# Loading the first weight groups in halves, with a new order of the opening stage

## The chip, the cores and the metric

The kernel runs on one core of a Trainium2 chip (trn2). The metric is the device time of one execution in microseconds; times are medians of several runs. A core has a matrix engine (TensorE, PE in the profile, with its weight loads as PEld), VectorE (DVE), ScalarE (ACT), GpSimd (POOL) and SyncE (SP), whose queue issues nearly all DMAs here.

## The reference

Three parts follow each other. Windowed attention over 4 batches and 8 heads (576 positions, head size 64), the lower four heads with a window of 32, the upper four with every fourth of 128; then a feed-forward layer with a maximum of three products; then a sum over eight experts, weighted by a matrix that is normalised eight times by rows and columns.

```python
scores = scale * np.matmul(q, k.transpose(0, 1, 3, 2))
scores = np.where(masks[None, :, :, :], scores, -1000000000.0)
attn = np.exp(scores - np.max(scores, axis=-1, keepdims=True))
attn = attn / (np.sum(attn, axis=-1, keepdims=True) + 1e-09)
out = np.matmul(attn, v)
...
h = np.maximum(np.maximum(x @ w1, x @ w2), x @ w3)      # 2304 x 512 by 512 x 768, weights in float64
x = (h @ w_out).astype(np.float32)
...
for e in range(E):                                       # E = 8, F = 1024
    h = np.maximum(x @ w1[e], 0.0)
    out += P[:, e:e + 1] * (h @ w2[e])
```

## The kernel before

The attention of batch 0 is computed in an opening stage of its own, four pairs of heads p = 0 to 3. The attention of batches 1 to 3 is spread over the feed-forward units of the batch before (`hooks`). Then come the experts' products, which fill most of the time. The change touches only the opening.

**Loads.** LOADS is a list of words that are issued in this order on SP's queue before any other work: `k` is keys and queries of a pair, `v` its values, `m` the two parts of the mask, `w` the small gate weight, `g` a group of feed-forward weights. The weights of the feed-forward layer are 64-bit numbers; a group holds two chunks of 128 x 512 of them, read as 32-bit words into a tile `cx` of 8 KB in a partition. There are three such tiles; group 3 needs the tile of group 0, and so on.

**Narrowing.** `narrow_ops` turns 64-bit numbers into a pair of 32-bit tiles (high part and remainder) in nine steps c1 to c9, each needing the one before: c1, c3, c4, c6, c7 and c9 on DVE, c2, c5 and c8 on ScalarE. In the opening, chunks 0 to 3 (groups 0 and 1) run through these steps one chunk at a time: c30 is step c3 of chunk 0. Index 4 stands for the whole of group 2, whose first two steps are in the opening too.

**Attention steps of pair p.** S: mask products and scores on PE; M: the row maxima on DVE; X: the exponentials on ScalarE; Ra, Rb: the sums' reciprocals on DVE and the normalisation on POOL; T0 to T2: three groups of three transposes on PE, each evacuated by E0 to E2 on ScalarE or DVE as EVAC says; V0, V1: the products with the values; H and L: the split of a result into a high part (ScalarE) and a remainder (DVE). The name is step, pair, part: T02 is the third group of pair 0, V31 the second half of pair 3; in T02+1 one filler product goes ahead of it.

**Order.** ORDER is written out by hand: within `with tc.manual_schedule()` every engine takes its instructions in the order of the list. An instruction that waits holds up all behind it on its engine. Outside that list PE's order stays that of the program, while the other engines' instructions are placed by a scheduler and may go between the items of the list. `keep_warm` issues filler products on PE ahead of the list. Pairs 1 and 2 take their score tiles from the same four PSUM buffers as the V products; transposes have two buffers of their own.

Behind the list, the first two groups' narrowed values are written back to memory (L778), which frees nothing but goes ahead of group 3's load on SP's queue, and `up(0, 0)` begins: units of 12 products (L443), each with an evacuation by ScalarE (L449) or DVE (L451). The unit 0 needs the split results of all four pairs and chunk 0; units 1 and 2 need chunks 1 and 2.

Of the kernel before, what the change touches and what calls it, by code (L numbers as in the profile page):

```python
# [9 lines left out]
F32 = mybir.dt.float32  # L10
F32R = mybir.dt.float32r
U32 = mybir.dt.uint32
# [5 lines left out]
B, H, S, D = 4, 8, 576, 64  # L18
# [23 lines left out]
STAGES = {0: "S Ma Mb Xe Ra Rb", 6: "W", 8: "T0 E0 T1 E1", 9: "T2 E2", 11: "V0 H0 L0 V1 H1 L1"}  # L42


LOADS = "m0 k0 w0 k1 m2 k2 g0 k3 v0 g1 v1 v2 v3 g2"
EVAC = "AAV VVV VAV AAA".split()
ORDER = (
# [5 lines left out]
)  # L53
NT, DM = B * S, H * D
F1 = 768
# [1 line left out]
P = 128  # L57
# [5 lines left out]
KT = DM // P  # L63
# [36 lines left out]
def attention_moe(ctx: ExitStack, tc: tile.TileContext, q, k, v, mask, wm1, wg, wm2, out):  # L100
    nc = tc.nc
# [13 lines left out]
    raw_p = ctx.enter_context(tc.tile_pool(name="raw", bufs=4))  # L115
    wa_p = ctx.enter_context(tc.tile_pool(name="wa", bufs=8))
    cx_p = tc.alloc_tile_pool(name="cx", bufs=3)
    dram = ctx.enter_context(tc.tile_pool(name="dram", bufs=1, space=bass.MemoryType.DRAM))
    ps_g = tc.alloc_tile_pool(name="ps_g", bufs=4, space=PSUM)
# [18 lines left out]
    def load_qk(b, p, pool):  # L138
        kt = pool.tile([P, S + WIN], F32, name="kt")
        qt = pool.tile([P, NQ, P], F32, name="qt")  # L140
        nc.sync.dma_start(kt, k[b, p])
        nc.sync.dma_start(qt, q[b, p])
        return qt, kt

    def load_v(b, p, pool):
        vt = pool.tile([KW, NQ, P], F32, name="vt")
        nc.sync.dma_start(vt, v[b, p])
        return vt

    def keep_warm(ps, n):  # L150

        for _ in range(n):
            nc.tensor.matmul(ps, ident[:, :ps.shape[0]], ident, start=True, stop=True)
# [209 lines left out]
    def fetch_w1(b, g):  # L363
        raw = raw_p.tile([P, 2, 512], F32, name="raw")
        if b:
            nc.sync.dma_start(raw, wm1f[g])
            return raw, None
        t = cx_p.tile([P, KT * S], U32, name="cx", tag="cx")
        nc.sync.dma_start(t[:, 0:2048].rearrange("p (i n) -> p i n", i=2), wm1[g].bitcast(U32))
        return raw, t  # L370
# [358 lines left out]
    qk, vs, raws = {}, {}, {}  # L729
    for what in LOADS.split():  # L730
        i = int(what[1])
        if what[0] == "k":
            qk[i] = load_qk(0, i, pools[i])
        elif what[0] == "v":
            vs[i] = load_v(0, i, pools[i])
        elif what[0] == "m":
            m0, m1 = (0, BANK0) if i == 0 else (BANK0, BANK0 + NQ * KW)
            nc.sync.dma_start(mraw[:, m0:m1], mask[:QT, m0:m1])
            if i == 0:
                nc.scalar.copy(mr[:QT, m0:m1], mraw[:, m0:m1])  # L740
        elif what[0] == "w":
            nc.sync.dma_start(wgr, wg)
        else:
            raws[i] = fetch_w1(0, i)
    steps = {"r2": lambda: nc.gpsimd.tensor_copy(mr[:QT, BANK0:], mraw[:, BANK0:])}
# [2 lines left out]
            if name not in "W X0 X1 X2 X3 X4 Ma Mb Xe".split():  # L748
                steps[f"{name[0]}{p}{name[1:]}"] = op
    first_w = made[0]  # L750
    keep_warm(ps_g.tile([P, 512], F32, name="ps")[:, 0:P], 8)
    todo = ORDER.split()
    raw, t = raws[2]
    parts = []
# [3 lines left out]
    for i in range(4):  # L758
        raw, t = raws[i // 2]
# [5 lines left out]
    with tc.manual_schedule():  # L765
        for name in todo:
            name, _, idle = name.partition("+")
# [328 lines left out]
    for i, (blk, e, n) in enumerate(stages):  # L1096
        wo, xo = w_ops.pop(i), x_ops[blk]
        raws = ahead_w.pop(i)
# [280 lines left out]
    for g in range((NBLK - 1) * E):  # L1379
        blk, e = 1 + g // E, g % E  # L1380
        sec = Second(blk, e, outs.pop(g))
        for n0 in range(0, NPAIR, 2):
            i = NS + g * NPAIR + n0
# [6 lines left out]
            ps = [[None, None], [None, None]]  # L1390
# [156 lines left out]
```

## Time and profile before

| | before |
|---|---|
| median of 3 runs | 1893.02 us (1892.87 to 1895.89) |
| profiled execution | 1894.94 us |
| its span, first to last instruction | 1893.0 us |
| mean granted TensorE clock | 0.992 |
| PE busy | 1852.9 us, 98% |
| DVE busy | 1335.1 us, 71% |
| ScalarE busy | 978.6 us, 52% |
| POOL busy | 648.7 us, 34% |

Times in the profile are microseconds from the start of the span. Busy times of a stretch are given for each engine; PEclk is the TensorE clock that was granted, 1.00 being 2.4 GHz and 0.50 being 1.2 GHz. A row of the timeline tells when an instruction (or a run of like ones, x their number) began, how long it took, its engine, line and operands, and in brackets how long the engine had been idle and what released it.

### The profile page before, as it was taken

To read this page: it belongs to the slowest core of one execution; us is meant where nothing else is said; L and a number is where in the kernel's file an instruction comes from. 1 tells how busy PE (TensorE), PEld (TensorE's weight loads), DVE (VectorE), ACT (ScalarE), POOL (GpSimd) and SP (SyncE) were. 2 spreads that over 40 slices of the span, in tenths; PEclk is the share of its full clock that TensorE was granted. 3 is DMA by queue.
4 is the path that set the end of the run, shared out by engine and by line. 5 is a ranking of instruction groups with operands and counts; after the bars stand their busy time and mean duration, and the time that the engine had idled before them with its cause. 6 is when DMAs were issued, how large, how long until landed. Compare 5 with 4: busy or idle time off the path is not lost.

```text
span 1893.0 us, 34127 instructions
## 1 busy us (share of the span) xinstructions
PE 1852.9 (98%) x12055; PEld 1745.3 (92%) x12055; DVE 1335.1 (71%) x2531; ACT 978.6 (52%) x2395; POOL 648.7 (34%) x552
## 2 busy tenths in 40 slices
PE   7899999999999999999999999999999999999998
PEld 6799999998899998989999999999989999999997
DVE  6993365677866677667587777877777677776777
ACT  5764445444554544454446555565545545555554
POOL 1123243335666676766512121121211211212111
PEclk8999999999999999999999999999999999999999
DMA  8776485866666668776977767777797676676763
GB/s 258 259 239 228 151 281 203 305 225 225 238 251 259 251 252 296 281 263 246 375 236 249 232 216 229 223 247 236 240 329 254 215 236 221 225 256 213 235 215 100
DMA packets 218441, 458.82 MB, mean 242 GB/s; under 512 B 19936, under 2 KB 102944, under 8 KB 216736
## 3 DMA queue, kind: packets, MB, share of 16 engines
q1 hardware_dynamic: 216640, 454.29, 70.6%
q10 hardware_dynamic: 1632, 2.36, 0.4%
q8 instruction: 96, 1.57, 0.3%
q14 instruction: 73, 0.60, 0.1%
HBM read 325.42 MB, written 130.81 MB: 241 GB/s over the span
## 4 chain that ended last, share of the span: by engine, by line
PE 82%; DVE 9%; DMA 4%; ACT 2%; issue 2%; POOL 1%; SPq 0%; DVEq 0%; ACTq 0%; POOLq 0%
PE po L1316 25%; PE po L1411 12%; PE po L1065 9%; PE ps L443 7%; PE p L1411 6%; PE q L1411 6%; PE q L1111 4%; PE p L1111 4%; PE ps L653 4%; DMA raw<-in_wm 1%; PE ps L573 1%; DVE sums L799 1%; DVE h L1162 1%; DVE ts L838 1%; DMA qt<-in_q 1%
## 5 line engine op out<-in xcount | busy, mean ns | idle before, releaser
L1316 PE MATMUL po<-wt,hop 128*128 128x256 f32 (+1 forms) x3264 | 482.9, 310 | 2.7 <-DMA wt<-wtd 2.7
L1316 PEld LDWEIGHTS po<-wt,hop 128*128 128x128 f32 x3264 | 444.9, 191 | 38.4 <-ACT wt L82 2.9
L83 POOL TENSOR_TENSOR wt<-raw,wt 128x256 fp32r<-128x256 f32 x192 | 186.4, 996 | 757.7 <-ACT wt L82 745.2
L83 DVE TENSOR_TENSOR hop<-r,hop 128x384 fp32r<-128x384 f32 x384 | 208.7, 573 | 188.6 <-ACT hop L82 184.8
L1065 PE MATMUL po<-wb,h 128*128 128x512 f32 x1152 | 295.0, 392 | 0.4 <-POOL wb L83 0.4
L1065 PEld LDWEIGHTS po<-wb,h 128*128 128x128 f32 x1152 | 213.4, 188 | 34.2 <-POOL wb L83 1.1
L82 ACT CAST hop<-r 128x384 fp32r<-128x384 f32 x384 | 188.7, 516 | 56.5 <-DVE r L1292 30.5
L443 PE MATMUL ps<-xt,wa 128*128 128x288 f32 x1296 | 187.0, 301 | 5.4 <-DVE xt L308 3.3
L443 PEld LDWEIGHTS ps<-xt,wa 128*128 128x128 f32 x1296 | 176.0, 190 | 9.2 <-DVE xt L308 3.8
L83 POOL TENSOR_TENSOR wa<-raw,wa 128x256 fp32r<-128x256 f32 (+1 forms) x107 | 130.9, 1228 | 110.7 <-ACT wa L82 87.7
L1425 ACT ACTIVATE r<-r 128x384 f32<-128x384 f32 x192 | 99.8, 525 | 128.9 <-DVE r L1424 128.0
L83 POOL TENSOR_TENSOR tw<-ts,tw 128x512 fp32r<-128x512 f32 x64 | 86.8, 1378 | 93.8 <-DVE h L1162 51.9
L1411 PE MATMUL po<-xB,wa 128*128 128x384 f32 x576 | 116.9, 338 | 0.0
L1411 PE MATMUL po<-xt,wa 128*128 128x384 f32 x576 | 116.9, 338 | 0.0
L1345 DVE SCALAR_TENSOR_TENSOR acc<-po,prob,acc 128x256 f32<-128x256 f32 x222 | 95.1, 475 | 21.6 <-PE po L1316 17.5
L83 POOL TENSOR_TENSOR wa<-sums,wa 128x512 fp32r<-128x512 f32 x64 | 88.0, 1394 | 51.5 <-ACT wa L82 32.9
L1411 PEld LDWEIGHTS po<-xB,wa 128*128 128x128 f32 x576 | 102.5, 188 | 0.0
L1411 PEld LDWEIGHTS po<-xt,wa 128*128 128x128 f32 x576 | 102.5, 188 | 0.0
L83 POOL TENSOR_TENSOR wb<-raw,wb 128x512 fp32r<-128x512 f32 x64 | 93.7, 1464 | 25.3 <-ACT wb L82 24.8
L1286 DVE TENSOR_TENSOR r<-r,r 128x384 f32<-128x384 f32 x128 | 93.2, 728 | 2.2
L799 DVE TENSOR_TENSOR sums<-raw 128x256 f32<-128x256 f32 x64 | 42.5, 663 | 68.6 <-DMA raw<-in_wm 68.6
L1327 ACT COPY mm<-po 128x256 f32<-128x256 f32 x144 | 49.6, 376 | 78.7 <-PE po L1316 78.7
(246 smaller groups left out, 3361.0 us busy)
## 6 DMA issues: line engine op xcount, KB each, us to landing
wa<-wsd SPq DMA_DIRECT2D x192, 512.0 KB, 4.3
wt<-wtd SPq DMA_DIRECT2D x256, 256.0 KB, 3.7
wsd<-wa SPq DMA_DIRECT2D x96, 512.0 KB, 3.3
raw<-in_wm SPq DMA_DIRECT2D x64, 512.0 KB, 4.3
wtd<-tw SPq DMA_DIRECT2D x128, 256.0 KB, 2.8
raw<-in_wm SPq DMA_DIRECT2D x128, 256.0 KB, 5.3
wa<-wsd SPq DMA_DIRECT2D x64, 256.0 KB, 4.6
cx<-in_wm SPq DMA_DIRECT2D x12, 1024.0 KB, 9.5
```

Source lines behind the costliest of these rows:

```text
L82: nc.scalar.copy(hi, src)
L83: sub.tensor_tensor(out=lo, in0=src, in1=hi.bitcast(F32), op=ALU.subtract)
L443: nc.tensor.matmul(ps, w[:, wi, kk], xt[:, xi, kk, n0:n0 + HB], start=(n == 0), stop=(n == 3 * KT - 1),)
L653: nc.tensor.matmul(ps, wo[f][:, wi, d2 * P:(d2 + 1) * P], hs[f][:, hi, a * HB:(a + 1) * HB], start=(f == 0 and n == 0), stop=(f == NF1 - 1 ...
L799: nc.vector.tensor_tensor(out=s[:, o], in0=x, in1=y, op=op)
L1065: nc.tensor.matmul(po, self.hs[f, j][:, hi, t * P:(t + 1) * P], self.ws[f][:, wi], start=(n + f + k == 0), stop=(n == NPAIR - 1 and f == 1 ...
L1111: nc.tensor.matmul(ps, wo[w][:, wi, kk], xo[x][:, xi, kk], start=(first and k == 0), stop=True if k == 5 else False, skip_group_check=not ...
L1286: nc.vector.tensor_tensor(out=r[o, n], in0=r[x, n], in1=r[y, n], op=op)
L1316: nc.tensor.matmul(self.ps[side, t][:, 0:x.shape[-1]], h[:, hi, t * P:(t + 1) * P], x, start=(first and i == 0), stop=(n == NPAIR - 1 and ...
L1345: nc.vector.scalar_tensor_tensor(out=a, in0=src, scalar=g, in1=a, op0=ALU.mult, op1=ALU.add)
L1411: nc.tensor.matmul(ps[k][side], wo[k][w][:, wi, kk], xo[x][:, xi, kk], start=(first and c == 0), stop=c == 5, skip_group_check=not first,)
L1425: nc.scalar.activation(out=r, in_=r, func=AF.Relu)
```

## The change

The two whole loads g0 and g1 become four half loads h0 to h3, one chunk of 512 KB each; the first stands directly behind the first part of the mask and the fourth behind the keys and queries of pair 1. Pair 1 is loaded ahead of pair 0, and the gate weight moves to the end of the list. ORDER is laid out anew: it begins with the narrowing of chunk 0 and the first step of chunk 3, the scores come in the order of pairs 1, 0, 2, 3, and the pairs' transposes, V products and splits are interleaved. The filler products ahead of the list go from 8 to 14. Chunks 0 and 3 are narrowed first, 1 and 2 later; the steps of group 2 (c14, c24) close the list.

```diff
-LOADS = "m0 k0 w0 k1 m2 k2 g0 k3 v0 g1 v1 v2 v3 g2"
+LOADS = "m0 h0 k1 h3 k0 m2 k2 k3 h1 h2 v1 v2 v0 v3 g2 w0"
 EVAC = "AAV VVV VAV AAA".split()
 ORDER = (
-    "S0 M0 X0 S1 M1 r2 R0a R0b X1 S2 M2 c10 c11 T02+1 T01 E02 c20 c21 E01 R1a R1b T00+2 E00 S3 X2 "
-    "c30 c40 c31 V01 V00 M3 R2a R2b c41 c50 T10 T11 E10 E11 T12 E12 c51 H01 H00 V11 V10 c12 X3 c60 c70 c61 "
-    "c71 R3a R3b c22 L01 L00 T20 E20 T21 E21 T22 E22 c80 H11 c81 H10 V21 V20 c90 c32 c42 L11 L10 c91 "
-    "T30+1 E30 T31 E31 T32 E32 c52 H21 H20 c62 L21 c72 L20 V31 V30 H31 c13 c82 H30 c23 L31 c92 c33 c43 "
-    "L30 c53 c14 c24 c63 c73 c83 c93"
+    "c10 c20 c30 c40 c50 c60 c13 S1 c70 M1 c23 c33 c43 c80 c90 S0 r2 S2 M0 X1 c53 R1a c63 X0 c73 M2 R1b "
+    "T11 c83 T12 R0a E11 c93 S3 E12 R0b T01 X2 c11 M3 c21 R2a c31 R2b T02+1 E01 E02 c12 c41 X3 T10 E10 "
+    "T20 V11 T21 E20 R3a T22 c22 E21 H11 c32 c51 R3b V20 E22 V21 H20 H21 L11 c61 c42 T00+2 T31 V10 c71 "
+    "E00 L20 E31 c52 L21 H10 T32 T30+1 V00 E32 E30 c62 c81 L10 c72 V31 H00 V30 c91 L00 H31 L31 H30 L30 "
+    "V01 H01 c82 L01 c92 c14 c24"
 )
...
         elif what[0] == "w":
             nc.sync.dma_start(wgr, wg)
+        elif what[0] == "h":
+            g, n = divmod(i, 2)
+            if g not in raws:
+                raws[g] = (
+                    raw_p.tile([P, 2, 512], F32, name="raw"), cx_p.tile([P, KT * S], U32, name="cx", tag="cx"),
+                )
+            nc.sync.dma_start(raws[g][1][:, n * 1024:(n + 1) * 1024], wm1[g][:, n].bitcast(U32))
         else:
             raws[i] = fetch_w1(0, i)
...
-    keep_warm(ps_g.tile([P, 512], F32, name="ps")[:, 0:P], 8)
+    keep_warm(ps_g.tile([P, 512], F32, name="ps")[:, 0:P], 14)
```

## Rows read from the trace of the kernel before

**Rows 1.** Stages: length, busy PE PEld DVE ACT POOL, PEclk, DMA share, GB/s.

```profile
5.00:10.00 5.00, 3.63 (x25) 2.72 (x23) 1.39 (x3) 0.92 (x6) 0.25 (x1) 1.00 1.03 275
10.00:15.00 5.00, 3.61 (x18) 3.64 (x18) 0.66 (x1) 2.32 (x15) 0.90 (x1) 0.66 1.02 375
15.00:20.00 5.00, 4.06 (x31) 3.24 (x30) 3.59 (x11) 3.84 (x20) 1.63 (x1) 1.00 1.06 293
35.00:40.00 5.00, 4.85 (x47) 3.78 (x45) 2.10 (x6) 2.69 (x8) 0.00 (x0) 0.50 0.99 308
```

**Rows 2.** The same view in stages of 10 us, around the hand-over from DVE to PE.

```profile
90.00:100.00 10.00, 8.46 (x105) 7.81 (x101) 9.85 (x17) 7.54 (x15) 1.87 (x1) 1.00 1.01 330
100.00:110.00 10.00, 9.95 (x102) 9.50 (x102) 10.00 (x20) 9.03 (x31) 1.64 (x1) 1.00 0.82 289
```

**Rows 3.** Timeline, the first landings and score products: start, us, engine line op.

```profile
1.79 3.45 PE L153 MATMUL ps<-ident 128*128 128x128 f32 x16 [1.79 <-POOL ident masks.py:199]
3.48 0.59 ACT L740 CAST mk<-mraw 64x480 fp32r<-64x480 f32 x1 [1.46 <-DMA mraw<-in_mask]
6.18 2.22 PE L190 MATMUL pss<-kt,qt 128*128 128x96 f32 x18 [0.36 <-DMA qt<-in_q]
11.39 3.85 PE L190 MATMUL ps<-kt,qt 128*128 128x96 f32 x18 [2.40 <-DMA qt<-in_q]
12.51 0.90 POOL L745 CAST mk<-mraw 64x864 fp32r<-64x864 f32 x1 [5.62 <-DMA mraw<-in_mask]
```

**Rows 4.** Timeline, narrowing steps of chunks 0 and 1 and a normalisation.

```profile
18.73 0.75 DVE L344 TENSOR_SCALAR raw<-cx 128x512 uint32<-128x512 uint32 x2
19.18 1.33 ACT L347 ACTIVATE raw<-raw,ebias 128x512 uint32<-128x512 uint32 x2
20.41 1.89 POOL L256 TENSOR_TENSOR sm<-sm,st 128x864 f32<-128x864 f32 x1 [2.27 <-DVE st L253]
20.85 1.74 DVE L351 TENSOR_SCALAR cx<-cx 128x512 uint32<-128x512 uint32 x1
24.80 0.37 DVE L351 TENSOR_SCALAR cx<-cx 128x512 uint32<-128x512 uint32 x1
28.16 0.69 DVE L358 TENSOR_TENSOR raw<-raw,cx 128x512 f32<-128x512 f32 x1
```

**Rows 5.** Timeline, V products and transposes, and the end of the opening.

```profile
23.69 1.27 PE L284 MATMUL ps<-pt,vt 96*64 96x64 f32 x36
24.89 0.86 PE L267 MATMUL pst<-ident,sm 128*96 128x128 f32 x6
29.89 1.52 PE L267 MATMUL pst<-ident,sm 128*96 128x128 f32 x6
38.79 1.98 PE L284 MATMUL ps<-pt,vt 96*64 96x64 f32 x32 [0.15 <-ACT pt L271]
45.41 0.61 PE L443 MATMUL ps<-xt,wa 128*128 128x288 f32 x2 [2.41 <-DVE xt L308]
45.26 1.29 DVE L344 TENSOR_SCALAR raw<-cx 128x1024 uint32<-128x1024 uint32 x2
47.80 2.35 DVE L348 SCALAR_TENSOR_TENSOR raw<-cx,raw 128x1024 uint32<-128x1024 uint32 x2
50.07 0.68 DVE L341 TENSOR_TENSOR wa<-raw,wa 128x512 fp32r<-128x512 f32 x1
```

**Rows 6.** DMA issues up to 60 us: op xcount, KB each, us to landing.

```profile
cx<-in_wm SPq DMA_DIRECT2D x6, 1024.0 KB, 12.1
qt<-in_q SPq DMA_DIRECT2D x6, 576.0 KB, 8.6
kt<-in_k SPq DMA_DIRECT2D x6, 304.0 KB, 7.2
mraw<-in_mask SPq DMA_DIRECT2D x1, 216.0 KB, 8.6
mraw<-in_mask SPq DMA_DIRECT2D x1, 120.0 KB, 2.7
```

## The prediction

> **What bounds the kernel now.** I read the table of stages first: engine time, granted TensorE clock and DMA rate in stretches of five and ten microseconds [rows 1]. Between 5 and 15 us VectorE (DVE) works 1.39 + 0.66 us of 10 while the DMA engines are full, so the kernel opens by waiting for its inputs. Past the opening the picture turns: between 90 and 100 us DVE is busy 9.85 of 10 and TensorE (PE) 8.46; from 100 us on PE is busy 9.95 of 10 [rows 2]. So the opening and the first 60 us of the feed-forward stage are limited by DVE (it narrows the 64-bit weights in the steps c1 to c9 and also evacuates PE's results), and the rest of the 1893 us by PE. What the change can win is therefore what DVE and PE have in hand when the opening ends, at about 45 to 50 us; nothing behind that is touched.
>
> The timeline shows how the opening runs. PE fills time with 16 small products until 5.2 us, then takes head pair 0 at 6.18, and pair 1 only at 11.39, released by the landing of its queries after 2.40 us of idling [rows 3]. DVE takes up the first weight step c1 at 18.73 [rows 4]. The opening ends with PE's first feed-forward unit waiting 2.41 us for the last DVE split L30 (45.41) and with DVE finishing c93 at 50.07 + 0.68 = 50.75 us. By then DVE has also done work that is not in ORDER: one of the two steps in the row at 45.26 (0.64 us) and both wide steps in the row at 47.80 (2.35) [rows 5]. Its own share of the opening thus ends at 50.75 - 3.0 = about 47.8 us. That is the figure to compare with.
>
> **When things land.** Bytes and queue are the same, only the order differs; the four half loads move what two whole ones did. Sizes are in [rows 6]. The landings of before give a curve of KB in queue order against time [rows 3]: m0 (120 KB) released ScalarE at 3.48; m0 + k0 (1000) released PE at 6.18; with w0 and k1 1896 KB at 11.39; with m2 2112 KB at 12.51. Past that I go on at 375 GB/s to 15 us, at 293 to 20 [rows 1], and by an estimate at the same 293 behind it. On this curve the new list lands: h0 (632 KB in all) at 5.05, k1 (1512) at 9.1, h3 (2024) at 12.05, k0 (2904) at 14.7, m2 at 15.3, k2 (4000) at 18.4, k3 at 21, h1 and h2 at 23 and 25. A half load has rows of 4 KB in place of 8; no row shows them apart. They lie between those of the keys and those of the whole loads, so I take the curve as it stands, with 1 us either way.
>
> **DVE's gain at the front.** A chunk costs DVE c1 0.375 (0.75 for two), c4 0.37, and c3, c6, c7, c9 at 0.69 each as the c7 row shows: 3.5 us; ScalarE's steps take 0.67 each (1.33 for two) [rows 4]. In the new order chunk 0 starts at 5.05 and comes to c60 at 5.05 + 0.375 + 0.67 + 0.69 + 0.37 + 0.67 + 0.69 = 8.5. There c13 stands in DVE's queue ahead of c70 and M1 and waits for h3 until 12.05: 3.5 us idle, with c70, M1 and everything else behind it, but M1 can't start before S1 is done at 11.4 anyway. Chunk 0 is complete at about 16. So 3.5 + 1.4 (c13, c33, c43) = 4.9 us of DVE work lies where DVE idled before. That is the most that can come out by this step alone.
>
> **PE's path.** The 6 added filler products are 12 instructions at 3.45 / 16 = 0.22 us [rows 3], 2.6 us, until 7.8; they lie in the wait for k1 (9.1) and cost nothing; if k1 came before 7.8 they would cost the difference. S1 then runs 9.1 to 11.4. S0 waits for k0 until 14.7. Before, idling of 2.40 us was followed by pair 1's products at half clock: 3.85 us in place of 2.22 [rows 3], clock 0.66 over 10 to 15 [rows 1]. The new gap is 3.3 us, so I take S0 at half clock, to 18.6; S2 with its 0.6 of mask products at half or full, to 21.4 or 23.1; T11 and T12 0.9; S3 2.9: 25.2 to 26.9. Then ten groups of transposes and four pairs of V products remain. At full clock a group is 0.86 / 2 = 0.43 us and a pair 1.27; at half clock 0.76 and 1.98 x 36 / 32 = 2.2 [rows 5].
>
> Which clock? From 35 to 40 us PE was busy 4.85 of 5 with nothing but such transposes and V products and the granted clock stayed at 0.50, the lower of its two levels, 1.2 GHz [rows 1]. So this kind of work doesn't bring the clock back, and with score products no longer among it I expect the fall soon after S3. The half-clock price is 10 x 0.76 + 4 x 2.2 + 0.7 of filler = 17.1; with the first two or three groups still at full clock, 16: PE ends at 41.2 to 44. Waits for evacuations add about 1: I take 43.7. At full clock throughout it is 10 x 0.43 + 4 x 1.27 + 0.4 = 9.8: PE would end at 35 to 36.7 and DVE would set the end.
>
> The Trainium skill (TensorE: Matmul & The Clock Gate, "Part 4: PE-mode transpose") says that transposes don't count as activity for the clock the way matmuls do. By that rule the new order's second half, mixing them with V products, stays at half clock; the trace agrees with its 0.50 over 35 to 40 us. By the opposite reading, where a busy PE is a fast PE, the full-clock sum would hold.
>
> **A stall that moves.** The normalisation Rb on GpSimd (POOL) ran from 20.41 for 1.89 us, and the c4 that DVE began at 20.85 took 1.74 us, ending with it, where the same step alone took 0.37 [rows 4]. In the new order every one of the four Rb has c steps beside it (c73, c93, c12, c32) where before one had. Each can cost up to 1.37 us, so the price is between 0 and 3 x 1.37 = 4.1 us more; most fall while DVE would wait for PE, and I count 0.8.
>
> The Trainium skill (SBUF — State Buffer, "Who interferes with whom") has the two engines share a port pair under an exclusive lock, for steps with two SBUF inputs as well. The 1.74 us of this c4 agrees; no run yet shows it for c7 or c9. It speaks against the change; by it the stall would come near 4.1, without it to 1.37 or less.
>
> **The sum.** Behind PE's end stand H01, L01, c92 and c14 on ScalarE and DVE: two splits and two steps at about 0.4, 0.4, 0.69 and 0.65, some 2.1 us. DVE's opening ends at 43.7 + 0.8 + 2.1 = 46.6 against 47.8: 1.2 us earlier. PE comes to its first unit 3 us later than before (43.7 against 38.79 + 1.98 = 40.8 [rows 5]), but before it could not finish that unit until 45.41 + 0.61, and it has gaps (1.5 us in 90 to 100 alone [rows 2]) to make up. The third group's load and the write-back wait for c71 and c72; the former DVE position of c61 and c71 was about 28 to 30 and is now about 35, but the queue has earlier loads until then. I take 1.0 us of the 1.2 through to the end.
>
> The profiled execution took 1894.94 us with a span of 1893.0, the median of the runs is 1893.02. The sum is a difference of spans; set against the median it gives 1893.0 - 1.0 = 1892.0.
>
> **The rivals.** (1) The clock holds: score products spread between transposes keep PE at 2.4 GHz to the end. PE's work, done by 36.7, is no longer last. DVE has 26 items of the list behind M3, which ends near 28 (S3, the evacuations and a stall): eleven c steps at 0.375 to 0.69, nine splits and two sums, four evacuations, by estimate 0.53 each, 13.7 us, without a wait: 42 us, 5.8 earlier, less about 0.8 for the next group's load landing late: 1888.0. For it: the clock was 1.00 over 15 to 20 us with the same mix; against it: 35 to 40 [rows 1]. A fall that comes late in the stage lands between, at about 1889.
>
> (2) The clock doesn't come back at all after the gap at 11.4. S2 and S3 take 3.85 each, PE reaches the end of V01 at about 47 and its first feed-forward units run at half clock: 47 + 2.8 by estimate, twelve products somewhat below the pace of the two in 0.61, = 49.8, where before it was 45.41 + 0.61 = 46.0 [rows 5]. PE is 4 us late: 1897. It decides from the point where PE's end of the opening passes about 45.5, when the later gaps no longer take it up. For it: the gap of 3.3 us. Against it: before, 3.85 us of score products brought the clock back.
>
> (3) The change doesn't do what it says: the half loads land no earlier (8 KB rows were cheaper, or the first 5 us are latency). Then c10 starts past 7, the gain at the front is 2 us less and the end stands as before: 1893.
>
> **How the numbers follow.** Forecast with (3), both within 0.2% (3.8 us, about what a measurement of this kernel can tell from no change): 0.50. Rival (1) with its late falls, to 1885 at the best landing: 0.31, most of it past 3.8 us: faster 0.30. Rival (2): 0.19, slower 0.18; what is left adds to same: 0.52. The range takes in the middle of (1) and the price of (2): 1886.5 to 1897. The likeliest case's own range is 1890 to 1894.5.
>
> **What would show it.** In the profile of after: c10 near 5 us and DVE waiting for h3 until 12; PE released by the queries of pair 1 near 9 and of pair 0 near 14.7; the granted clock of 28 to 43 (0.5 is my step, 1.0 rival 1) and of 15 to 26 (0.5 is rival 2); c steps beside an Rb at over 1.3 us; the end of L30 and c92 against 46. I am wrong if DVE is no longer busy past 95% up to 100 us, or if the loads of groups 3 and 4 land after DVE asks for them.

## The result and the profile after

The changed kernel takes 1906.42 us (median of 6 runs, 1905.48 to 1909.22), the kernel before 1893.86 us: a ratio of 1.0068, 95% interval 1.0055 to 1.0081. It is slower by 12.6 us; 1892.0 was forecast, and the range ended at 1897. The profiled execution took 1908.67 us with a span of 1906.7, that of before 1894.94 with 1893.0: 13.7 us more in both ways of counting.

Where the 13.7 us lie can be read from the start of each twelve-product unit of L443, the same units in the same order in both traces (unit 108 is the first behind them, of L573). The table gives this start in the changed kernel minus that in the kernel before, worked out from the timeline.

| unit | start before | after minus before |
|---|---|---|
| 1 | 47.75 | -1.49 |
| 4 | 53.24 | -2.09 |
| 7 | 61.54 | +1.92 |
| 8 | 63.49 | +6.08 |
| 13 | 79.61 | +1.86 |
| 16 | 87.53 | +6.12 |
| 24 | 106.89 | +4.77 |
| 25 | 109.32 | +11.02 |
| 31 to 47 | 121.84 | +11.95 |
| 48 | 174.64 | +10.62 |
| 108 | 340.79 | +13.59 |

In these two executions the opening is a success: units 1 to 4 start 1.5 to 2.1 us early. Then the stage loses 8 us by unit 8, takes 4 back by unit 13, loses them again by unit 16, and loses 6 us more at unit 25. All of that is at 55 to 120 us, behind the lines that the change edits.

The timeline of the opening in the changed kernel (start, us, engine, line, operation; in brackets the idle time and what ended it):

```profile
1.79 5.18 PE L153 MATMUL ps<-ident 128*128 128x128 f32 x28 [1.79 <-POOL ident masks.py:199]
6.36 0.43 DVE L344 TENSOR_SCALAR raw<-cx 128x512 uint32<-128x512 uint32 x1 [4.30 <-DMA cx<-in_wm]
8.92 2.22 PE L190 MATMUL ps<-kt,qt 128*128 128x96 f32 x18 [1.37 <-DMA qt<-in_q]
10.65 0.43 DVE L344 TENSOR_SCALAR raw<-cx 128x512 uint32<-128x512 uint32 x1 [0.49 <-DMA cx<-in_wm]
14.47 2.91 PE L190 MATMUL pss<-kt,qt 128*128 128x96 f32 x18 [2.75 <-DMA qt<-in_q]
18.32 4.15 PE L190 MATMUL ps<-kt,qt 128*128 128x96 f32 x18
18.65 1.88 POOL L256 TENSOR_TENSOR sm<-sm,st 128x864 f32<-128x864 f32 x1 [2.29 <-DVE st L253]
19.08 2.00 DVE L358 TENSOR_TENSOR raw<-raw,cx 128x512 f32<-128x512 f32 x1
```

These answer [rows 3] and [rows 4]. c10 starts at 6.36 us where the first weight step of before started at 18.73, and pair 1's scores start at 8.92 in place of 11.39. The last two rows are one event: c7 of chunk 3, 0.69 us alone [rows 4], takes 2.00 us beside the normalisation on POOL and ends 0.55 us behind it (21.08 against 20.53).

Stages of the changed kernel (length, then busy time of PE, PEld, DVE, ACT, POOL, granted clock, DMA share, GB/s):

```profile
30.00:35.00 5.00, 4.22 (x37) 3.15 (x37) 2.92 (x8) 1.53 (x8) 1.89 (x1) 0.50 1.00 287
35.00:40.00 5.00, 4.61 (x52) 4.09 (x54) 3.39 (x9) 3.67 (x11) 0.25 (x1) 0.53 0.44 141
40.00:45.00 5.00, 5.00 (x101) 4.64 (x96) 4.37 (x11) 4.45 (x13) 0.00 (x0) 1.00 0.98 338
60.00:70.00 10.00, 3.74 (x14) 3.39 (x15) 10.00 (x15) 7.19 (x26) 0.00 (x0) 0.68 0.69 260
80.00:90.00 10.00, 5.00 (x33) 4.72 (x33) 10.00 (x14) 6.82 (x21) 0.00 (x0) 0.87 0.62 210
90.00:100.00 10.00, 10.00 (x129) 9.65 (x129) 9.99 (x17) 7.96 (x19) 2.40 (x1) 0.95 0.97 342
110.00:120.00 10.00, 4.25 (x30) 3.98 (x30) 10.00 (x19) 6.77 (x23) 3.92 (x1) 0.91 0.39 141
120.00:130.00 10.00, 10.00 (x87) 9.67 (x86) 5.99 (x10) 5.14 (x13) 0.00 (x0) 0.75 0.00 0
```

Two of these stages in the kernel before:

```profile
60.00:70.00 10.00, 8.43 (x60) 7.50 (x59) 10.00 (x16) 5.37 (x11) 1.64 (x1) 1.00 0.98 348
110.00:120.00 10.00, 10.00 (x104) 9.77 (x102) 10.00 (x17) 6.74 (x17) 0.00 (x0) 1.00 0.72 259
```

This is the picture that misleads. PE was busy 8.43 us of 10 in 60 to 70 us and 10.00 in 110 to 120; now it is busy 3.74 and 4.25. Yet DVE, the engine that bounds this stretch, is busy 10.00 of 10 in both stages, before and after. It isn't short of work; it works on what PE doesn't need yet. What PE waits for, 45 to 130 us of the changed kernel (engine, tile, line, releaser: total, times, longest):

```profile
PE pst L267 <- POOL sm L256: 5.7, 1, 5.7
PE ps L443 <- ACT wa L337: 5.0, 1, 5.0
PE pst L267 <- DVE xt L308: 5.0, 1, 5.0
PE ps L443 <- DVE wa L341: 2.8, 1, 2.8
PE pss L184 <- DMA qt<-in_q: 1.2, 1, 1.2
PE pst L267 <- ACT pt L271: 0.3, 1, 0.3
```

They sum to 20.0 us, against 11.1 us in the same view of the kernel before, of which 2.4 end at 45.41, still inside unit 0. Four waits make 18.6 of them. They are found in PE's timeline:

```profile
63.47 0.75 PE L443 MATMUL ps<-xt,wa 128*128 128x288 f32 x2 [5.03 <-ACT wa L337]
67.01 4.71 PE L443 MATMUL ps<-xt,wa 128*128 128x288 f32 x22 [2.80 <-DVE wa L341]
88.23 1.48 PE L267 MATMUL pst<-ident,sm 128*96 128x128 f32 x6 [5.00 <-DVE xt L308]
119.17 1.51 PE L267 MATMUL pst<-ident,sm 128*96 128x128 f32 x6 [5.75 <-POOL sm L256]
```

Unit 7 is the first that uses a tile of group 2. Its first product waits for the high part, c8 (L337); its third is the first that needs the remainder and waits for c9 (L341). With the long waits come times at half clock: 0.68 over 60 to 70 us, 0.87 over 80 to 90, 0.75 over 120 to 130. A mean of 0.68 means 6.4 of 10 us at 0.50. Worked out in this way, the last five rows of the changed kernel give 16.8 us at half clock; in the kernel before, 3.4 of 45 to 50 us (clock 0.66) and 3.4 of 70 to 80 us (0.83). The clock is the smaller part of the loss all the same. From the end of unit 0 to the start of unit 31 the changed kernel takes 12.6 us longer (45.35 to 133.79 us, before 46.02 to 121.84). PE's busy time in this stretch is 68.42 us, before 67.08, so 1.3 us are slower work and 11.3 us are idle time.

Why is the weight late although DVE never rests? DVE's timeline in the changed kernel; L344, L355, L358, L341 are c1, c6, c7, c9:

```profile
51.68 0.69 DVE L344 TENSOR_SCALAR raw<-cx 128x1024 uint32<-128x1024 uint32 x1 [0.16 <-DMA cx<-in_wm]
54.87 2.49 DVE L348 SCALAR_TENSOR_TENSOR raw<-cx,raw 128x1024 uint32<-128x1024 uint32 x1
57.28 1.21 DVE L355 SCALAR_TENSOR_TENSOR cx<-cx 128x1024 f32<-128x1024 uint32 x1
61.55 1.21 DVE L358 TENSOR_TENSOR raw<-raw,cx 128x1024 f32<-128x1024 f32 x1
66.28 1.28 DVE L341 TENSOR_TENSOR wa<-raw,wa 128x512 fp32r<-128x512 f32 x2
68.69 0.68 DVE L341 TENSOR_TENSOR wa<-raw,wa 128x512 fp32r<-128x512 f32 x1
71.54 1.75 DVE L341 TENSOR_TENSOR wa<-raw,wa 128x512 fp32r<-128x512 f32 x1
```

and in the kernel before:

```profile
55.37 0.68 DVE L344 TENSOR_SCALAR raw<-cx 128x1024 uint32<-128x1024 uint32 x1
57.10 1.22 DVE L358 TENSOR_TENSOR raw<-raw,cx 128x1024 f32<-128x1024 f32 x1
61.31 1.28 DVE L341 TENSOR_TENSOR wa<-raw,wa 128x512 fp32r<-128x512 f32 x2
```

The first row of each is c1 of group 4. In the changed kernel it stands at 51.68, ahead of the c6 and c7 of group 2; before, it stood behind group 2's c6. So three groups (2, 3, 4) advance abreast and their last steps all lie between 66.28 and 73.29: the rows of L341 at 66.28, 68.69 and 71.54 belong to groups 2, 3 and 4. Before, the c9 of group 2 stood at 61.31, 5 us earlier. Of these 5 us, 1.3 are the c3 of group 4 in the row at 54.87, which took 2.49 us in place of 1.21 beside an Rb on POOL (from 54.65, 1.63 us). The sum of DVE's work is hardly larger: up to 120 us it was busy 102.7 us, before 100.9.

### The profile page after: what moved, and what is told of

The parts are those of the page before. It is cut to its first block, busy times and chain, and to the rows that moved or that the text cites. A ratio compares the mean times of both kernels' runs of the same rounds, so it can differ in the third digit from the quotient of the medians.

```text
span 1906.7 us, 34156 instructions
## 1 busy us (share of the span) xinstructions
PE 1854.8 (97%) x12067; PEld 1749.4 (92%) x12067; DVE 1336.6 (70%) x2531; ACT 981.4 (51%) x2395; POOL 651.2 (34%) x552
## 4 chain that ended last, share of the span: by engine, by line
PE 82%; DVE 8%; DMA 6%; ACT 2%; issue 2%; POOL 1%; SPq 0%; DVEq 0%; ACTq 0%; POOLq 0%
PE po L1323 25%; PE po L1418 12%; PE po L1072 9%; PE ps L443 7%; PE p L1418 6%; PE q L1418 6%; PE q L1118 4%; PE p L1118 4%; PE ps L653 3%; DMA raw<-in_wm 1%; PE ps L573 1%; DVE sums L806 1%; DVE ts L845 1%; DVE h L1169 1%; DMA cx<-in_wm 1%
## 5 line engine op out<-in xcount | busy, mean ns | idle before, releaser
L443 PE MATMUL ps<-xt,wa 128*128 128x288 f32 x1296 | 188.0, 302 | 7.8 <-ACT wa L337 5.0
L443 PEld LDWEIGHTS ps<-xt,wa 128*128 128x128 f32 x1296 | 177.7, 192 | 10.7 <-ACT wa L337 5.3
```

Of the source, the lines that this page charges most:

```text
L443: nc.tensor.matmul(ps, w[:, wi, kk], xt[:, xi, kk, n0:n0 + HB], start=(n == 0), stop=(n == 3 * KT - 1),)
```

## The experiments

Twelve kernels ran, in three sets; each set shares runs of the kernel before, whose median was 1894.61, 1894.70 and 1893.95 us. Ratios are against these.

**Is it the opening or the sequence behind it?** The placement of the feed-forward instructions on DVE and ScalarE, which nobody wrote by hand, differs between the two builds. In e1 and e2 it is prescribed: each of the 213 instructions of DVE and 227 of ScalarE gets an edge from the one ahead of it, in the sequence that the other kernel's build had.

```diff
+            own = [x for x in traced if str(x.engine).endswith(name)]
+            for i, j in zip(at, at[1:]):        # at: the other build's sequence
+                tc.add_manual_dep(own[j], own[i].name, ..., reason="order")
```

e1, the new opening with the feed-forward sequence of before:

> The changed kernel, with the 213 VectorE and 227 ScalarE instructions of the feed-forward stage of batches 0 and 1 put back into the sequence they have in the kernel before (order edges only, no added work). Theory A: the loss is that the change altered that sequence, and the opening itself gained some 2 us. Then the unit that waited at 58.4 to 67.0 us waits under 2 us, and the time is 1889 to 1894, about that of before or 1 to 4 us less. Rival B: the loss is in the opening (its loads, clock or buffers), and the sequence only follows it. Then the time stays near 1906, within 3 us.

1897.17 us, ratio 1.0010 (0.9999 to 1.0021): the loss is gone, but the time lies above theory A's 1889 to 1894, and a gain of the opening doesn't show.

e2, the old opening with the feed-forward sequence of the changed kernel:

> The kernel before with its own loads and opening, but with those 213 and 227 instructions in the sequence of the changed kernel. Theory A: it is slow as well, 1903 to 1911 (10 to 17 us over before), with TensorE waiting over 5 us for group 2's weights and twice again later. Rival B: it stays within 3 us of before, 1891 to 1897.

1907.73 us, ratio 1.0068 (1.0046 to 1.0090), the loss of the change itself, with the opening of before. Its units stand at +6.17 (8), +9.77 (25) and +9.67 us (48), like those of the changed kernel. The two together settle it: the loss is the sequence behind the opening. With the old sequence the new opening can't be told from the old one.

**What in the sequence?** e3 keeps the changed kernel and adds one rule, with all else left to the scheduler:

```diff
+            if name == "c1" and g - 2 in narrowed:
+                with tc.issue_after(narrowed[g - 2]):    # c9 of the group two ahead
+                    op()
```

> The changed kernel with one rule added in the feed-forward stage: VectorE's first step of group g stands behind its last step of group g-2, so that at most two weight groups are in narrowing at once. Theory A in its narrower form (three groups narrowed in step, so that none is done when TensorE needs it): half or more of the 13 us comes back, 1890 to 1899. If another part of the sequence than the number of groups in progress does it, or under rival B: 1902 to 1908.

1895.06 us, ratio 0.9996 (0.9985 to 1.0007). Keeping a third group from starting takes away the whole loss. Its loads of groups 3 and 4 are issued at 37.18 and 41.44 us, as close together as in the changed kernel; so near loads do no harm by themselves, their steps being let in does. The same rule on the kernel before is the control:

> The kernel before with the rule of e3: VectorE's c1 of a group may only be placed behind c9 of the group two ahead of it. A control for e3: if the rule by itself gave several us, then e3 (0.9996 of the kernel before) would hide a loss of that size that remains in the new opening. Theory A: the rule changes little where the sequence is staggered anyway, 1891 to 1896 us. Rival: the rule itself gains, 1885 to 1889.

1894.96 us, ratio 1.0007 (0.9995 to 1.0019): the rule gains nothing by itself that could hide a loss in e3. Its trace also warns how to read unit starts. With the old opening unit 1 starts at 42.84 us, 4.9 earlier than in the trace of before and earlier than in the changed kernel; by unit 48 the lead is 2.2. The granted clock differs too: up to 45 us it was 0.50 for 10.2 us there (30.42 to 37.25 and 40.66 to 44.08) and for 17.1 in the trace of before (11.58 to 14.99 and 28.65 to 42.30). How much of the lead is the clock isn't separated.

**The fillers.** e4 is e1 with 8 filler products in place of 14:

> As the first run, but with 8 filler products in place of 14. If the fillers only lie in the wait for pair 1 and its clock: TensorE's first scores of pair 1 start at the same time, at most at the lower clock for 1.6 us longer, and the end is within 2 us of the first run. If the clock in the opening decides (the fall comes earlier and stays): 3 us or more above the first run.

1896.93 against e1's 1897.17: no difference in the time. In the one traced execution of e4 the scores of pair 1 took 4.13 us, in that of e1 2.22, and unit 1 starts 3.8 us later than in e1; whether the fewer fillers did that isn't shown by one trace of each.

**Which part of the change calls up the bad sequence?** e5 moves four words of the new list:

```diff
-    "E00 L20 E31 c52 L21 H10 T32 T30+1 V00 E32 E30 c62 c81 L10 c72 V31 H00 V30 c91 L00 H31 L31 H30 L30 "
-    "V01 H01 c82 L01 c92 c14 c24"
+    "E00 L20 E31 c52 L21 H10 T32 T30+1 V00 E32 E30 c81 L10 V31 H00 V30 c91 L00 H31 L31 H30 L30 "
+    "V01 H01 L01 c14 c24 c62 c72 c82 c92"
```

> The changed kernel with one edit: in ORDER the steps c62 c72 c82 c92 of the third half chunk (group 1) go from among the transposes to the end, behind c24. Loads, fillers and everything else stay. c72 is the last reader of group 1's raw tile before its write-back, so the load of group 4 (42.54 us in the changed kernel, 4.3 us behind that of group 3) can only start later. The sequence that is built for VectorE behind the opening then has the first step of group 4 behind group 2's c7, no longer ahead of it. Theory A2 (the feed-forward sequence was lost because group 4's weights became ready too early, which let its steps in among those of groups 2 and 3): 1891 to 1897 us, units 25 to 30 no more than 1 us behind the kernel before, where the changed kernel is 11 to 13 us behind. Rival (the sequence is a matter of the opening's length or of group 3's load alone): 1903 to 1908, as changed.

1896.91 us, ratio 1.0012 (1.0002 to 1.0022). Units 8, 25 and 48 stand at -0.18, +0.52 and -0.29. Of the 12.6 us excess, 2.2 are left. The issue rows of SyncE's queue show the step: first in the changed kernel (write-backs of groups 0 and 1, each followed by a load into the buffer that comes free, of groups 3 and 4), then the write-back of group 1 and the load of group 4 in e5, then that load in the kernel before:

```profile
37.88 0.33 SPq L785 DMA_DIRECT2D wm1f<-raw  x1
38.26 0.42 SPq L369 DMA_DIRECT2D cx<-in_wm  x1
42.16 0.33 SPq L785 DMA_DIRECT2D wm1f<-raw  x1
42.54 0.43 SPq L369 DMA_DIRECT2D cx<-in_wm  x1
```

```profile
46.39 0.33 SPq L785 DMA_DIRECT2D wm1f<-raw  x1
48.08 0.49 SPq L369 DMA_DIRECT2D cx<-in_wm  x1
```

```profile
48.29 1.23 SPq L369 DMA_DIRECT2D cx<-in_wm  x1
```

Group 4's load leaves behind the write-back of group 1, which waits for c72. In the changed kernel it leaves at 42.54; in e5 at 48.08, close to the 48.29 of the kernel before. e6 and e7 ask whether it is this time or the distance between the two loads that counts. Both complete group 0 first (loads h0 h1 h2 h3, steps of chunks 0, 1, 2, 3), and differ in four words only:

```diff
-    "E00 L20 E31 c53 L21 H10 T32 T30+1 V00 E32 E30 c63 c82 L10 c73 V31 H00 V30 c92 L00 H31 L31 H30 L30 "
-    "V01 H01 c83 L01 c93 c14 c24"
+    "E00 L20 E31 c53 L21 H10 T32 T30+1 V00 E32 E30 c82 L10 V31 H00 V30 c92 L00 H31 L31 H30 L30 "
+    "V01 H01 L01 c14 c24 c63 c73 c83 c93"
```

e6 (with +, the steps late):

> The changed kernel with the quarters renamed so that group 0 is complete first (loads h0 h1, then h2 h3; steps of chunk 0, 1, 2, 3 in this sequence), and c63 c73 c83 c93 at the end behind c24. Group 0's write-back and with it the load of group 3 then come near 20 us in place of 38, that of group 4 near 50. Theory A2: the sequence of VectorE is staggered as in the kernel before and the load of group 3 no longer ends a wait (in e1 VectorE idled 1.6 us for it), so 1889 to 1895 us. Rival: what the opening gives is taken back at unit 15 whatever is done, because VectorE's work is the same: 1893 to 1897.

1897.10 us, ratio 1.0020 (1.0006 to 1.0034). The loads of groups 3 and 4 leave at 27.07 and 45.30 us and the sequence is staggered, but the time is 0.1 us above the rival's range: DVE waits 1.5 us for loads where it was 1.6 in e1.

e7 (with -, the steps early):

> As e6, but c63 c73 c83 c93 stay among the transposes, where the changed kernel has them. The loads of groups 3 and 4 are then issued some 20 us apart (in the changed kernel 4.3, in the kernel before 17.7), but the second of them as early as in the changed kernel, near 42 us. The sequence built for VectorE again has the first steps of groups 2, 3 and 4 next to one another. Theory A2 (what counts is how early group 4 is ready): 1902 to 1908 us, units 8 and 9 about 6 us behind. Rival A3 (what counts is the distance of the two loads, or that group 3's load was late): 1891 to 1896.

1901.01 us, ratio 1.0035 (1.0020 to 1.0050). The loads of groups 3 and 4 are issued at 26.90 and 39.51 us, 12.6 apart in place of 4.3, and three groups go abreast again; units 8 and 25 are at +2.29 and +6.65. So a wider distance doesn't heal it, though the rival said so; but the loss of 6.3 us is half of the changed kernel's 12.6, and the time just below the range of the theory. With e3 and e5 this shows that group 4's steps, ready early, are what spoils the sequence; by what rule they are placed was read from the built sequences only, and how much the late load of group 3 adds to the price isn't separated.

**Where does the opening's gain go?** In e1 unit 13 starts 6.72 us earlier than in the kernel before, and unit 16 0.20 us later. Not all of this lead is the new order's, since executions differ in their clock: with the same opening list unit 0 starts at 40.79 us in e1, behind 10.2 us at half clock, and at 43.47 in the changed kernel, behind 17.1. In the trace of e1 this is the place where the lead is lost (lines are 17 higher than before: L273 is Rb, L372 c6, L325 a split, L284 a transpose):

```profile
77.28 1.87 POOL L273 TENSOR_TENSOR sm<-sm,st 128x864 f32<-128x864 f32 x1 [16.35 <-DVE st L270]
77.58 2.65 DVE L372 SCALAR_TENSOR_TENSOR cx<-cx 128x1024 f32<-128x1024 uint32 x1
80.16 0.48 DVE L325 TENSOR_TENSOR xt<-pso,xt 128x320 fp32r<-128x320 f32 x1
80.78 1.72 PE L284 MATMUL pst<-ident,sm 128*96 128x128 f32 x6 [6.03 <-DVE xt L325]
```

PE is early, but waits 6.03 us for a split that stands in DVE's sequence behind weight steps, one of them taking 2.65 us beside Rb in place of 1.21. My reading was that DVE's amount of work is the limit. e9 takes 4.2 us of it away in the same sequence: c7 of groups 3 to 6 works on 8 of its 1024 columns and leaves their weights unmultiplied.

```diff
-            "c7": lambda: nc.vector.tensor_tensor(out=dst, in0=dst, in1=mf, op=ALU.mult),
+            "c7": lambda: nc.vector.tensor_tensor(out=dst[:, :few], in0=dst[:, :few], in1=mf[:, :few], op=ALU.mult),
```

> As e1 (the new opening, VectorE's and ScalarE's feed-forward sequence as in the kernel before), but c7 of the groups 3 to 6 works on 8 of its 1024 columns, so four instructions of 1.21 us become short, the sequence staying the same. Their weights are left unmultiplied. Theory (the gain of the opening vanishes in e1 because from 50 to 120 us VectorE's work is the limit): the stage gets back up to 4 x 1.1 = 4.4 us, so 1892.5 to 1895 against e1's 1897.17. Rival (TensorE or the loads are the limit there): 1896 to 1898, as e1.

1895.91 us, ratio 1.0004 (0.9992 to 1.0016), 1.3 us below e1 with intervals that overlap. It lies between the two expectations. The waits of DVE from 45 to 120 us in e9 show what became of the time (L361 is c1, L365 c3, L358 c9, L269 Ra):

```profile
DVE raw L361 <- DMA cx<-in_wm: 2.8, 1, 2.8
DVE st L269 <- ACT sm L254: 1.0, 1, 1.0
DVE raw L365 <- ACT raw L364: 0.8, 2, 0.6
DVE wa L358 <- ACT wa L354: 0.7, 1, 0.7
```

DVE is busy 69.6 us of these 75 in place of 72.8 in e1 (74.7 before): it now waits for a group's load, and for ScalarE. So it isn't DVE's work alone; that a group's load, which has to wait for a buffer and then for the queue, stands right behind it is a reading of these waits. Unit 19 starts at 97.14 us before, 0.19 earlier in e1 and 0.10 earlier in e9. A fourth `cx` buffer would tell the two apart; it wasn't tried.

**A version that beats both?** e10 to e12 give the second c9 of each group from group 3 on to GpSimd, on the kernel before, on e6 and on e5. The sequence of the other steps is left to the scheduler and may change too:

```diff
+                eng = second if second is not None and i else nc.vector    # second: nc.gpsimd
+                eng.tensor_tensor(out=w[:, 1], in0=x, in1=w[:, 0].bitcast(F32), op=ALU.subtract)
```

> The kernel before with the second c9 of every weight group from group 3 on given to GpSimd. VectorE loses 9 steps of 0.767 us between 45 and 125 us, 6.9 us in all; GpSimd takes 1.39 us for one (the 128x512 subtraction elsewhere in the kernel), during which a two-input step of VectorE may stand still: at most 9 x 1.39 = 12.5 us given back. If VectorE's work is the limit and half of the steps collide: 1893.0 - 6.9 + 6.2 = about 1892, between 1888 and 1896. Rival (the collisions are total): 1898. Rival (TensorE is the limit): 1893, whatever VectorE does.

1897.59 us, ratio 1.0017 (1.0007 to 1.0027), above the range of the first expectation and nearest in time to the rival with the total collisions. Groups of DVE's instructions from 45 to 125 us in e10 (L349 is c3, L342 c9, L352 c4, L356 c6; busy, mean ns of one):

```profile
L349 DVE SCALAR_TENSOR_TENSOR raw<-cx,raw 128x1024 uint32<-128x1024 uint32 x9 | 13.5, 1504 | 0.3 <-ACT raw L348 0.3
L342 DVE TENSOR_TENSOR wa<-raw,wa 128x512 fp32r<-128x512 f32 x9 | 10.5, 1172 | 0.0
L352 DVE TENSOR_SCALAR cx<-cx 128x1024 uint32<-128x1024 uint32 x9 | 7.6, 844 | 0.0
L356 DVE SCALAR_TENSOR_TENSOR cx<-cx 128x1024 f32<-128x1024 uint32 x8 | 9.7, 1211 | 0.0
```

In the kernel before these means were 1350, 767, 694 and 1375 ns. Nine c9 that stay take 0.40 us longer each, nine c3 0.15, nine c4 0.15: 6.4 us. Eight c6 take 0.16 less each, 1.3 us, so 5.1 us came back, where the seven steps that POOL did in this stretch freed 7 x 0.767 = 5.4. Nearly all of the work that was moved came back as longer steps; the collisions weren't total, the 6.4 us being well under the 11.0 us that POOL was busy with its seven.

> e6 (quarters in their own order, the last one behind the opening) with the second c9 of every group from group 3 on given to GpSimd. If the opening's gain in e6 was taken back because VectorE's work is the limit up to 120 us, then with 6.9 us less of it the gain should show as far as GpSimd's holding of the shared port allows: 1890 to 1895 against e6's 1897.1. Rival: collisions cost more than 6.9 us: 1898 to 1902.

1895.45 us, ratio 1.0005 (0.9992 to 1.0017): just above the range of the first expectation, below e6, and not told apart from the kernel before.

> e5 (the changed kernel with c62 c72 c82 c92 at the end of the list) with the second c9 of every group from group 3 on given to GpSimd. As e11: 1890 to 1895 against e5's 1896.9 if VectorE's work is the limit and few steps collide; 1898 to 1902 if the collisions cost more than the 6.9 us that are moved.

1901.09 us, ratio 1.0043 (1.0026 to 1.0061): the rival's range. Whether collisions or a changed sequence cost more here isn't separated. None of the twelve is measurably faster than the kernel before.

## Why the prediction was wrong

**The step that failed** is half a sentence: "nothing behind that is touched". The sum took the opening's end, carried 1.0 us of it to the end of the kernel, and left the feed-forward stage as it was. But DVE's instructions outside the list are placed by a scheduler, and the prediction had even counted three of them ahead of the list's last step [rows 5]. A new opening gives that scheduler another start, above all another time for group 4's load, and it lays out the next 70 us anew. The span came out 13.7 us longer, although units 1 to 4 came up to 2.1 us early.

**The marks nearly missed it.** The prediction named as signs of an error DVE below 95% before 100 us, and loads that land after DVE asks. DVE fell below 95% in one stage only, 70 to 80 us, with 8.47 us of 10, behind the first loss and not at its cause; the load of group 4 made DVE wait 0.16 us (51.68). The mark should have been what PE waits for, and which group's step DVE does at that time.

**"The third group's load and the write-back wait for c71 and c72"** was written down, with the price of a later load in mind. What decided was the opposite case, group 4's load 5.75 us earlier (42.54 against 48.29), which looked like a gift.

**The opening's own steps held well.**

| step | predicted | measured |
|---|---|---|
| h0 lands, c10 starts | 5.05 | 6.36 |
| S1 starts (k1) | 9.1 | 8.92 |
| h3 lands, c13 | 12.05 | 10.65 |
| S0 starts (k0) | 14.7 | 14.47 |
| fillers end | 7.8 | 6.97 |
| unit 0 can start | 43.7 | 43.47 |
| last item of DVE's opening ends | 46.6 | about 46.3 (c14, in the row at 45.61) |

The curve of bytes was right within 1.4 us, its stated 1 us being a little narrow. DVE waited for h3 0.49 us where 3.5 was counted, since h0 came later and h3 earlier. Rival 3 is refuted by c10 at 6.36. The instructions of the filler products took 0.185 us each (5.18 / 28) where 0.22 was counted. That PE reached unit 0 at 43.47 for a forecast of 43.7 is partly luck. Behind S3, which ended at 26.03 as forecast, it waited 3.4 us (0.32, 1.95 and 1.14) where about 1 was counted, and its work took about 14 us where 16 was.

**The clock** was granted at 0.50 from 15.81 to 22.64 us and from 29.47 to 39.71. S0 fell into the first with 2.91 us, between the full-clock 2.22 and the 3.85 that was counted, and S2 paid 4.15; S3, from 23.78 on, was at full clock. The second fall "soon after S3" is as predicted, but the clock returned at 39.71, among transposes, V products and two filler products, which I had said don't bring it back; over 40 to 45 us it was 1.00 with PE busy 5.00 of 5. The stage 35 to 40 of the kernel before, 0.50 with PE busy 4.85 [rows 1], was thus no rule about the kind of work. Rival 2 is refuted, and rival 1 holds for the last 4 us only.

**Stalls beside Rb** were counted at 0.8 us out of 0 to 4.1. Measured: c7 at 19.08 lost 1.31 us (2.00 for 0.69), c1 at 25.00 0.95 (1.38 for 0.43), c1 at 28.87 0.96. That is 3.2 us of DVE time, near the upper bound. DVE then waited 0.86, 1.05, 1.64 and 1.26 us up to 40.44 us, so part of it would have been idle anyway; how much isn't shown. The Trainium skill (SBUF — State Buffer, "Who interferes with whom") says that a DVE step with two SBUF inputs contends with a GpSimd instruction that reads SBUF, and calls the ports that the two share an exclusive lock. The 2.00 us of c7 agree, and so do the c9 of e10. Both c1 have one input and were held as well.

**The rival that came nearest** in its time is the slower one, 1897 with a chance of 0.19, by another mechanism. None of the rivals changed the sequence; a chance for it, priced from the spread of what DVE's steps cost when they are not those that PE needs next (one group's steps ahead of the wanted ones: 0.68 + 1.35 + 0.69 + 1.38 + 1.21 + 2 x 0.77 = 6.9 us by their means between 45 and 125 us of the kernel before), would have put the range's upper end near 1900 (1893.0 + 6.9), still short of 1906.

**What stays open.** From unit 48 to unit 108 the changed kernel loses another 3.0 us, e5 1.15 and e6 2.06. In the changed kernel PE waits 1.1 and 0.7 us for `xg` (L698) just ahead of unit 108, where it waited 0.3 before; the cause wasn't tested. The stretch at half clock at 353.73 to 357.14 us begins only 0.65 us ahead of that unit. The lead of the first units is lost between units 13 and 19 in e1, e5 and e9; that DVE's work alone is not the reason is shown by e9, that the loads' buffers are the rest is only argued.

## What to carry to other kernels

Where part of an order is written by hand and the rest is placed by a scheduler, an edit of the written part is an edit of the whole: compare the built sequences behind it before costing it at nothing. A load that comes free earlier is no gain if its first steps go ahead of steps that a consumer needs sooner; an engine busy 100% can starve the next one, so read the waits of the consumer and not the busy share of the bound. Holding work back by one rule (e3) or by four words in a list (e5) took away nearly all of a loss of 12.6 us.

## What the runs showed of the hardware

Blocking between DVE and POOL goes both ways. In the changed kernel one Rb, 1.68 us on average in the kernel before, took more than twice that:

```profile
115.19 3.92 POOL L256 TENSOR_TENSOR sm<-sm,st 128x864 f32<-128x864 f32 x1 [18.16 <-ACT h L82]
```

It began while DVE ran two c9 (115.21, 1.28 us) and a c3 (116.41, 1.21 us), and the next two c9 beside it took 2.35 us in place of 1.28. This Rb ends the 5.75 us wait of PE at 119.17, the step from +4.77 to +11.02 between units 24 and 25. The collision is 2.2 us of that wait (3.92 against 1.68); the rest is that its reciprocal stood late in DVE's sequence (114.82). In e2, with the same sequence, the same Rb took 3.93 us and PE waited 5.7. In e10 5.4 us of work that went from DVE to POOL came back as 5.1 us of longer steps on DVE.

The granted clock differs between executions with the same opening list: 0.50 for 17.1 us ahead of unit 0 in the changed kernel, in e3 and in e9, and for 10.2 us in e1, which reached that unit 1.7 to 2.7 us earlier.
